# Attention of the later batches in fewer, longer visits to TensorE, with the transposed input loaded twice

## The chip, the cores and the metric

The kernel runs on one core of one Trainium2 chip. The metric is device time in microseconds (us): the median of 3 runs of the kernel before is 1649.5 us (1649.0 to 1649.99).

## The reference

Two stages follow each other. The first is an attention through 32 inducing points, for 4 batches of 12480 tokens with 128 channels; the second is a feed-forward layer over all 49920 tokens.

```python
def mab(q, kv):
    s = scale * (q @ kv.transpose(0, 2, 1))
    s = s - s.max(-1, keepdims=True)
    a = np.exp(s)
    a /= a.sum(-1, keepdims=True) + 1e-09
    return a @ kv

h = mab(inducing, x)          # 32 x 128 for each batch: every token is weighted
out = mab(x, h)               # 12480 x 128 for each batch: 32 scores a token
hid = out @ w_in              # 128 -> 2048
g = hid / (1 + exp(-1.702 * hid))
result = g @ w_out            # 2048 -> 128
```

All is float32, to float32 accuracy.

## The kernel before

**Tiling.** A batch is cut into super-blocks (`sups`, line 82): six of 4 x 512 tokens and a last one of 2 x 96; `NS` is 7. Attention works by super-block, the feed-forward layer by block of 512 tokens: 24 blocks for each batch, and one block for the rests of two batches together. Each block takes 8 steps (`NG`), one for each pair of 128-wide chunks of the 2048 hidden channels, so the main loop at line 751 has 784 steps.

**The feed-forward step.** `first(i)` (line 650) issues two 512-column products into `ph` (a PSUM pair, two of them in rotation), then ScalarE computes the gate `g`, ScalarE or VectorE a rounded copy `hi`, and VectorE the rest `lo`. `second(i, c)` (line 677) issues three products, hi with wl, lo with wh, hi with wh, into `pso`, for one of the two chunks: one half step. So a step is eight 512-column products. Half steps are issued late by `lag` halves; `lag` grows by one every `EXTRA` = 3 steps up to `LAG[1]` and is thrown back to `LAG[0]` = 6 when the attention yields `LUMP` (a run of exponentials on ScalarE with two loads of its function table); the halves over 6 are then issued at once, so TensorE has work while ScalarE is away. `ph_` holds the pairs hi and lo.

**The first layer's weights.** `hT` of a batch times `w_in` gives `hw[b, c]` for four quarters c (`h_w_in`, line 486): a product of TensorE, a copy of ScalarE, a subtraction of VectorE. The list `products` (line 727) says at which step each quarter is issued, counted from the first step that needs it: for batches 1 and 3 that is the block of rests. `phw` holds six such tiles. With them the feed-forward layer works on the attention's weights of a token (laid out as stacks `st` by `weights_of`, line 501, through DMA) and never builds the attention's output.

**The attention as a generator.** `attention(b)` (line 197) yields after each small piece; the main loop advances it by one piece a step (line 776), after the step's `first` and its halves. So whatever it issues to TensorE stands between two feed-forward steps: a visit. `hop(n)` and, in the later batches, `wait(n)` yield n times. For the batches 1 to 3 (`start` is false) its order is:

1. load the transposed input, one super-block a step (`load_xT`, line 158; 1 MB each): seven loads, six tiles `xt` in rotation (`px`) and one small tile `xt_last`;
2. `first_scores(s)` for each super-block: a visit of four 512-column products to the 32 columns of a quarter of the array each, which the trace records as eight; VectorE copies the scores from PSUM and reduces their maximum one step later; two more steps pass;
3. the maximum over the batch (`maximum`), then the exponentials of four super-blocks and a `LUMP`; the other three follow in the third super-block of item 4;
4. the weighted sum: for each of 25 pieces (`pieces`, 4 blocks of 32 x 4 tokens, 3 in the last) `load_x` (line 167) brings the untransposed input three pieces ahead in four DMAs of 64 KB, `weigh` (line 280) issues four products of 128 columns (eight in the trace) and two steps pass;
5. the normalisation gives `hT`;
6. `second_scores(s)` for each super-block, in two groups of 3 and 4: a visit like that of item 2 from the same `xt` tiles, VectorE's transpose and maximum, GpSimd's subtraction, and at the group's end the exponentials and a `LUMP`.

`full()` (line 133) holds the score visits back while no score tile is free; there are nine, given back by `aT_of` and `weights_of`.

**The first batch** (`start`) has no feed-forward work beside it. Its loads, scores, transposes (`turn_x`, line 180) and the splitting of the weights (`weights`, line 564) fill the first 70 us; five `xt` loads go out first, alternating with the four of `w_in`, and x4 is among them. In it the weighted sum already runs by whole super-blocks. Its second scores of super-blocks 2 to 6 fall into the main loop.

**Queues.** All DMAs are issued by SyncE in the order of the program: an instruction that waits there holds up all behind it, the stores of `outT` (line 775) and the stack tiles (line 541) among them. Every engine works its own instructions in program order.

Of the kernel before, what the change touches and what calls it, by code (L numbers as in the profile page):

```python
# [8 lines left out]
F32 = mybir.dt.float32  # L9
# [10 lines left out]
BLK = TOK // 32  # L20
XC = 4
RG = 2
LAG = 6, 10
EXTRA = 3
# [3 lines left out]
SPIN = 9, 20  # L28
ES = 5
FB = 5  # L30
LEAST = 2.0 ** -15
# [24 lines left out]
def set_attention_then_moe(ctx: ExitStack, tc, xT, x, indT, w_in, w_out, outT):  # L56
# [34 lines left out]
    const = ctx.enter_context(tc.tile_pool(name="const", bufs=1))  # L91
    px = ctx.enter_context(tc.tile_pool(name="px", bufs=NS - 1))
    pe = ctx.enter_context(tc.tile_pool(name="pe", bufs=EB))
    pt = ctx.enter_context(tc.tile_pool(name="pt", bufs=7))
    pst = ctx.enter_context(tc.tile_pool(name="pst", bufs=G))
    phw = ctx.enter_context(tc.tile_pool(name="phw", bufs=6))
    psm = ctx.enter_context(tc.tile_pool(name="psm", bufs=3))
# [34 lines left out]

    def full():
        return len(held) >= EB and not held[-EB]

# [30 lines left out]

    def load_x(b, s, c):

        t0, g, w = sups[s]
        n = min(XC, w // 32 - c * XC)  # L170
        t = pn.tile([P, XC, P], F32, tag="xn", name="xn")
        for j in range(g):
            r0 = b * N + t0 + j * w + c * XC * 32
            nc.sync.dma_start(
                t[32 * j:32 * j + 32, 0:n],
                x[r0:r0 + 32 * n, :].rearrange("(k i) c -> i k c", i=32),
            )
        return t
# [18 lines left out]
    def attention(b):  # L197
# [3 lines left out]
        if not start:  # L201
            for s in range(NS):
                load_xT(b, s)
                yield
# [7 lines left out]

        def first_scores(s):
            t0, g, w = sups[s]
            while s < NS - 1 and full():
                yield
            pa = ps_a.tile([P, 512], F32, tag="pa", name="pa")
            xg = xts[b, s][:, 0:g * w]
            if start:
                xg = xg.rearrange("c (k g i) -> c g k i", g=g, i=32)  # L220
            else:
                xg = xg.rearrange("c (g t) -> c g t", g=g)
            for j in range(g):
                pe_.matmul(
                    pa[32 * j:32 * j + 32, 0:w], indT_sb, xg[:, j], start=True, stop=True
                )
            yield
            q = 32 * g
            e, slot = take("s1", s)
            if start:  # L230
                act.copy(e[0:q, 0:w], pa[0:q, 0:w])
                dve.tensor_reduce(mx[0:q, s:s + 1], pa[0:q, 0:w], axis=AX.X, op=ALU.max)
            else:
                dve.tensor_copy(e[0:q, 0:w], pa[0:q, 0:w])
                dve.tensor_reduce(mx[0:q, s:s + 1], e[0:q, 0:w], axis=AX.X, op=ALU.max)
            s1[s] = e, slot

        def maximum(n):
# [40 lines left out]

        def weigh(pa, s, c, xn, i, n):  # L280

            t0, g, w = sups[s]
            q = 32 * g
            for kk in range(min(XC, w // 32 - c * XC)):
                j = i % G
                pe_.matmul(
                    pa[32 * j:32 * j + 32, 0:P], aTs[s][0:q, XC * c + kk, :], xn[0:q, kk],
                    start=(i < G), stop=(i >= n - G),
                )
                i += 1  # L290
            return i

        hu = psm.tile([P, P], F32, tag="hu", name="hu", bufs=1)
        rs1 = psm.tile([P, 1], F32, tag="rs1", name="rs1")
        pieces = [(s, c) for s in range(NS) for c in range(-(-sups[s][2] // (32 * XC)))]

# [3 lines left out]
        if start:  # L300

            turned = {}
            for s in range(ES):
                if s < 4:
                    squares()
                    fill(6 if s else 5)
                    if s < NS - ES:
                        load_xT(b, s + ES)
                yield from first_scores(s)
                if s > 0:  # L310
                    turned[s - 1] = turn_x(b, s - 1)
            squares()
            pace[0] = 1
# [9 lines left out]
            aT_of(4)  # L323
            turned[ES - 1] = turn_x(b, ES - 1)
            squares()
            fill(FILLS[0])
# [13 lines left out]
            for s in range(ES):  # L340
                for c in [c for r, c in pieces if r == s]:
                    i = weigh(
                        h1, s, c, turned[s][:, XC * c:], i, blocks(range(ES))
                    )
                if s == 0:
                    next(whole)
                    fill(FILLS[1])
                    next(whole)
                if s == 2:
                    next(whole)  # L350
                    fill(FILLS[2])
                    next(whole)
                    next(whole, None)
                if s == 1:
                    turned[ES] = turn_x(b, ES)
                    squares()
            nmx2 = found[0]
# [4 lines left out]
            for s in range(ES, NS):  # L362
                if s not in turned:
                    turned[s] = turn_x(b, s)
                for c in [c for r, c in pieces if r == s]:
                    i = weigh(
                        h2, s, c, turned[s][:, XC * c:], i, blocks(range(ES, NS))
                    )
            fill(FILLS[3])
# [9 lines left out]
        else:  # L379
            for s in range(NS):  # L380
                yield from first_scores(s)
                yield from wait(2)
# [5 lines left out]
            pa = ps_a.tile([P, 512], F32, tag="pa", name="pa")  # L388
            xq = pieces
            loaded = {}  # L390
            aT_of(0)
            for k in range(3):
                loaded[k] = load_x(b, *xq[k])
            yield from wait()
            i = 0
            for k, (s, c) in enumerate(xq):
                if c == 0 and s == 2:
                    for r in range(4, NS):
                        first_exponential(r, nmx)
                    yield LUMP  # L400
                if c == 1 and s + 1 < NS:
                    aT_of(s + 1)
                if k + 3 < len(xq):
                    loaded[k + 3] = load_x(b, *xq[k + 3])
                i = weigh(pa, s, c, loaded.pop(k), i, blocks(range(NS)))
                yield from wait(2)
            dve.tensor_copy(hu, pa[:, 0:P])
# [20 lines left out]

        def second_scores(s):

            t0, g, w = sups[s]
            q = 32 * g
            while s < NS - 1 and full():
                yield
            pa = ps_a.tile([P, 512], F32, tag="pa", name="pa")
            for j in range(g):
                pe_.matmul(
                    pa[32 * j:32 * j + 32, 0:w], hT[:, 0:M], xts[b, s][:, j * w:(j + 1) * w],
                    start=True, stop=True,
                )  # L440
            yield
            e, slot = take("e", s)
            k = w // 32
            e = e[:, 0:w].rearrange("p (k m) -> p k m", m=M)
            dve.transpose(e[0:q].rearrange("p k m -> p (k m)"), pa[0:q, 0:w])
            m2 = psm.tile([P, BLK], F32, tag="m2", name="m2")
            dve.tensor_reduce(m2[0:q, 0:k], e[0:q], axis=AX.X, op=ALU.max)
            yield
            eng = dve if start and s == 0 else nc.gpsimd
            eng.tensor_sub(e[0:q], e[0:q], m2[0:q, 0:k].unsqueeze(2).broadcast_to([q, k, M]))  # L450
            yield
            return e, slot
# [8 lines left out]
        if start:  # L461
            for s in range(2):
                mine[s] = yield from second_scores(s)
                exponentials(s, mine[s])
# [10 lines left out]
        yield  # L475
        turn = list(range(NS)) if b % 2 == 0 else [NS - 1, *range(NS - 1)]
        for some in (turn[2:],) if start else (turn[0:3], turn[3:]):
            yield from hop(20 if start else 8)
            for s in some:
                mine[s] = yield from second_scores(s)  # L480
            yield
            for s in some:
                exponentials(s, mine[s])
            yield LUMP
# [217 lines left out]
    with tc.tile_pool(name="pf", bufs=FB) as pf, tc.tile_pool(name="pw", bufs=2) as pw:  # L702
        dec = weights()
        for s in range(ES):
            if s < 4:
                load_w(w_in, s * WC)
            load_xT(0, s)
# [7 lines left out]
    po = ctx.enter_context(tc.tile_pool(name="po", bufs=2))  # L715
    pn = ctx.enter_context(tc.tile_pool(name="pn", bufs=4))

# [10 lines left out]
    for b in range(1, B):  # L728
        f = first_block[b, NS - 1 if b % 2 else 0] * NG
        products += [(f + at, b, c) for c, at in enumerate((-4, -2, 1, 3) if b % 2 else (-7, -5, -3, -1))]  # L730
    rest = attentions()
# [85 lines left out]
```

## Time and profile before

| | |
|---|---|
| time of the profiled execution | 1648.21 us |
| span inside it | 1646.4 us |
| median of 3 runs | 1649.5 us |
| TensorE matmul busy | 1609.2 us, 98% |
| VectorE busy | 1394.4 us, 85% |
| ScalarE busy | 1326.5 us, 81% |
| GpSimd busy | 202.4 us, 12% |
| DMA moved | 101.53 MB, mean 62 GB/s |

Matmuls are pipelined: a product of 512 columns is shown with some 400 ns while the next starts about 230 ns after it, so the busy time counts overlaps once and says only that TensorE is hardly ever idle. What a visit costs is therefore read from starts: from the start of one product to the start of the same product a few steps later. "x8" in a row is eight records merged; a score or weighing product in full float32 is recorded twice.

### The profile page before, as it was taken

Reading aid. Unit: us, or ns where it says so; the run is one execution under the profiler, and the core shown is the slowest. Engines: PE = TensorE matmul, PEld = TensorE weight load, DVE = VectorE, ACT = ScalarE, POOL = GpSimd, SP = SyncE. Lnnn points to the kernel's source line nnn. Section 1 sums busy time; section 2 is a strip of 40 time slices with the busy share of each in tenths; the row PEclk is TensorE's granted clock in tenths of the full one; section 3 lists DMA queues with packets and bytes.
Section 4 is the critical chain, followed back from the end, with each engine's and each line's share of the span. In section 5 each row is a group of like instructions: output and inputs, shape, how many; then the busy total and the mean of one; then the engine's idle time right before and its main releaser. Section 6 shows DMA issues by size and latency. Waiting matters only on the chain.

```text
span 1646.4 us, 22186 instructions
## 1 busy us (share of the span) xinstructions
PE 1609.2 (98%) x7737; PEld 1222.0 (74%) x7737; DVE 1394.4 (85%) x1526; ACT 1326.5 (81%) x1502; POOL 202.4 (12%) x134
## 2 busy tenths in 40 slices
PE   6799999999999999999999999999999999999999
PEld 4477777777777877777777777777777888888887
DVE  7798977878988898788988987877989888888886
ACT  6588788878887888878888778887788888888886
POOL 4321110102211011010120110110122001101100
PEclk9999999999999999999999999999999999999999
DMA  6105113311041112330105101322101011011010
GB/s 259 26 26 189 39 48 94 96 36 45 18 149 71 37 46 60 98 93 23 39 20 194 41 26 51 96 78 67 39 23 33 27 45 46 20 39 45 20 46 20
DMA packets 81950, 101.53 MB, mean 62 GB/s; under 512 B 14704, under 2 KB 53168, under 8 KB 78768
## 3 DMA queue, kind: packets, MB, share of 16 engines
q1 hardware_dynamic: 81840, 100.11, 19.5%
q8 instruction: 63, 1.03, 0.3%
q14 instruction: 47, 0.39, 0.1%
HBM read 48.94 MB, written 25.56 MB: 45 GB/s over the span
## 4 chain that ended last, share of the span: by engine, by line
PE 84%; DVE 3%; ACT 2%; issue 1%; DVEq 0%; ACTq 0%
PE pso L46 59%; PE ph L46 21%; PE pa L46 4%; DVE lo L46 2%; ACT g L46 1%; DVE hi L46 1%; ACT hi L46 0%; ACT L46 0%; DVE hw L46 0%; ACT e L46 0%; DVE sm L46 0%; ACT s L46 0%; DVE e L46 0%; ACT ob L46 0%; DVE m L46 0%
## 5 line engine op out<-in xcount | busy, mean ns | idle before, releaser
L46 DVE TENSOR_TENSOR lo<-g,hi 128x1024 fp32r<-128x1024 f32 (+1 forms) x784 | 985.4, 1266 | 155.6 <-ACT hi L46 142.0
L46 ACT ACTIVATE g<-ph 128x1024 f32<-128x1024 f32 (+1 forms) x784 | 804.1, 1029 | 258.5 <-PE ph L46 129.8
L46 PE MATMUL pso<-hi,wl 128*128 128x512 f32 (+1 forms) x1568 | 622.5, 397 | 0.0
L46 PE MATMUL pso<-hi,wh 128*128 128x512 f32 (+1 forms) x1568 | 616.2, 393 | 0.0
L46 PE MATMUL pso<-lo,wh 128*128 128x512 f32 (+1 forms) x1568 | 615.6, 393 | 0.0
L46 PE MATMUL ph<-st,hw 128*128 128x512 f32 x1536 | 495.9, 404 | 8.0 <-ACT g L46 4.4
L46 ACT ACTIVATE hi<-ph 128x1024 fp32r<-128x1024 f32 x453 | 462.6, 1021 | 0.0
L46 PEld LDWEIGHTS ph<-st,hw 128*128 128x128 f32 x1536 | 276.8, 188 | 117.5 <-ACT hi L46 27.2
L46 PEld LDWEIGHTS pso<-lo,wh 128*128 128x128 f32 x1568 | 293.9, 187 | 72.5 <-issue 2.4
L46 PEld LDWEIGHTS pso<-hi,wl 128*128 128x128 f32 x1568 | 294.4, 188 | 69.9 <-issue 2.9
L46 PEld LDWEIGHTS pso<-hi,wh 128*128 128x128 f32 x1568 | 294.3, 188 | 70.0
L46 DVE CAST hi<-g 128x1024 fp32r<-128x1024 f32 (+1 forms) x331 | 248.5, 751 | 65.0 <-ACT g L46 64.3
L513 POOL TENSOR_TENSOR e<-e,sm 128x512 f32<-128x512 f32 (+1 forms) x27 | 43.1, 1598 | 1164.2 <-DVE sm L46 922.1
L46 ACT COPY ob<-pso 128x512 f32<-128x512 f32 (+1 forms) x98 | 57.9, 590 | 21.5 <-PE pso L46 20.9
L450 POOL TENSOR_TENSOR e<-e,m 128x512 f32<-128x512 f32 (+1 forms) x27 | 49.7, 1840 | 163.5 <-DVE m L46 163.5
L517 POOL TENSOR_TENSOR e<-e,ah 128x512 f32<-128x512 f32 (+1 forms) x27 | 48.9, 1812 | 2.2
L46 PE MATMUL pa<-xt,indT_sb 128*32 128x512 f32 x192 | 28.2, 661 | 11.0 <-DMA xt<-in_xT 11.0
L46 ACT ACT_TABLE_LOAD x28 | 35.9, 1283 | 1.2 <-PEq L807 0.7
L46 PE MATMUL pa<-xn,aT 128*32 128x128 f32 (+1 forms) x594 | 31.9, 285 | 0.0
L46 PEld LDWEIGHTS pa<-xn,aT 128*32 128x32 f32 (+1 forms) x594 | 11.8, 107 | 26.9 <-issue 23.6
L516 POOL CAST ah<-e 128x512 fp32r<-128x512 f32 (+1 forms) x27 | 28.2, 1043 | 1.7
L46 PE MATMUL pa<-xt,hT 128*32 128x512 f32 x192 | 27.0, 641 | 1.0 <-DVE hT L46 1.0
(97 smaller groups left out, 436.0 us busy)
## 6 DMA issues: line engine op xcount, KB each, us to landing
xt<-in_xT SPq DMA_DIRECT2D x24, 1024.0 KB, 9.9
out_T<-ob SPq DMA_DIRECT2D x96, 256.0 KB, 2.0
xn<-in_x SPq DMA_DIRECT2D x288, 64.0 KB, 1.9
st<-ahT SPq DMA_DIRECT2D x192, 64.0 KB, 2.0
st<-alT SPq DMA_DIRECT2D x192, 64.0 KB, 2.0
raw<-in_w_in SPq DMA_DIRECT2D x4, 512.0 KB, 8.9
raw<-in_w_out SPq DMA_DIRECT2D x4, 512.0 KB, 12.5
xt_last<-in_xT SPq DMA_DIRECT2D x4, 96.0 KB, 10.8
```

The costliest lines, as they stand in the source:

```text
L46: return f(*a, **k)
L450: eng.tensor_sub(e[0:q], e[0:q], m2[0:q, 0:k].unsqueeze(2).broadcast_to([q, k, M]))
L513: eng.tensor_mul(e[0:q], e[0:q], sm[0:q, 0:nb].unsqueeze(2).broadcast_to([q, nb, M]))
L516: eng.tensor_copy(ah[0:q, 0:w], e2[0:q])
L517: eng.tensor_sub(e2[0:q], e2[0:q], ah[0:q, 0:w].bitcast(F32))
```

## The change

**The weighted sum goes by super-blocks.** `load_x(b, s)` brings a whole super-block of x (1 MB in four DMAs of 256 KB, two tiles in rotation), one super-block ahead; `weigh` issues all its 16 blocks in one visit, and six steps pass between visits instead of two. So 7 visits a batch take the place of 25.

**Scores go by pairs.** `first_scores` is split into `first_products` and `first_out`, `second_scores` into `second_products` and `second_out`. For the batches 1 to 3 two super-blocks' products are issued in one visit and their outputs follow two steps apart; `full(n)` asks for n free score tiles. The second scores' groups become 4 and 3. For batch 0 the pairs apply to the second scores of super-blocks 2 to 6.

**Four xt tiles** (`XB`) instead of six. Super-blocks 4 and 5 are loaded when the products of 0 and 1 are out; all six are loaded a second time (`again`) for the second scores, four during the weighted sum, two during the second scores. A later batch therefore starts with four loads in four steps, not seven in seven. In batch 0, x4 and x5 are loaded after the transposes of super-blocks 0 and 1.

**Smaller edits.** `LAG` is 6, 12 instead of 6, 10 and `ph_` one pair larger; `phw` has seven tiles; for batches 1 and 3 the products of `hT` with `w_in` are issued at steps -6, -4, -2, 1 instead of -4, -2, 1, 3. The hunks left out below are the rest of the split of `first_scores` and the two calls of `weigh` in batch 0.

```diff
@@ -18,15 +18,15 @@
 BLK = TOK // 32
-XC = 4
 RG = 2
-LAG = 6, 10
+LAG = 6, 12
 EXTRA = 3
 ES = 5
+XB = 4
 FB = 5
@@ -89,11 +89,11 @@
     const = ctx.enter_context(tc.tile_pool(name="const", bufs=1))
-    px = ctx.enter_context(tc.tile_pool(name="px", bufs=NS - 1))
+    px = ctx.enter_context(tc.tile_pool(name="px", bufs=XB))
     pe = ctx.enter_context(tc.tile_pool(name="pe", bufs=EB))
     pst = ctx.enter_context(tc.tile_pool(name="pst", bufs=G))
-    phw = ctx.enter_context(tc.tile_pool(name="phw", bufs=6))
+    phw = ctx.enter_context(tc.tile_pool(name="phw", bufs=7))
     psm = ctx.enter_context(tc.tile_pool(name="psm", bufs=3))
@@ -130,8 +130,9 @@

-    def full():
-        return len(held) >= EB and not held[-EB]
+    def full(n=1):
+
+        return any(len(held) + k >= EB and not held[len(held) + k - EB] for k in range(n))

@@ -164,16 +165,15 @@

-    def load_x(b, s, c):
+    def load_x(b, s):

         t0, g, w = sups[s]
-        n = min(XC, w // 32 - c * XC)
-        t = pn.tile([P, XC, P], F32, tag="xn", name="xn")
+        t = pn.tile([P, BLK, P], F32, tag="xn", name="xn")
         for j in range(g):
-            r0 = b * N + t0 + j * w + c * XC * 32
+            r0 = b * N + t0 + j * w
             nc.sync.dma_start(
-                t[32 * j:32 * j + 32, 0:n],
-                x[r0:r0 + 32 * n, :].rearrange("(k i) c -> i k c", i=32),
+                t[32 * j:32 * j + 32, 0:w // 32],
+                x[r0:r0 + w, :].rearrange("(k i) c -> i k c", i=32),
             )
@@ -199,7 +199,7 @@
         if not start:
-            for s in range(NS):
+            for s in range(XB):
                 load_xT(b, s)
...
@@ -235,6 +236,11 @@

+        def first_scores(s):
+            pa = first_products(s)
+            yield
+            first_out(s, pa)
+
         def maximum(n):
@@ -277,14 +283,14 @@

-        def weigh(pa, s, c, xn, i, n):
+        def weigh(pa, s, xn, i, n):

             q = 32 * g
-            for kk in range(min(XC, w // 32 - c * XC)):
+            for kk in range(w // 32):
                 j = i % G
                 pe_.matmul(
-                    pa[32 * j:32 * j + 32, 0:P], aTs[s][0:q, XC * c + kk, :], xn[0:q, kk],
+                    pa[32 * j:32 * j + 32, 0:P], aTs[s][0:q, kk, :], xn[0:q, kk],
                     start=(i < G), stop=(i >= n - G),
@@ -292,7 +298,16 @@
         rs1 = psm.tile([P, 1], F32, tag="rs1", name="rs1")
-        pieces = [(s, c) for s in range(NS) for c in range(-(-sups[s][2] // (32 * XC)))]
+        turn = list(range(NS)) if b % 2 == 0 else [NS - 1, *range(NS - 1)]
+
+        def pairs(some):
+            some = list(some)
+            return [some[k:k + 2] for k in range(0, len(some), 2)]
+
+        def again(s):
+
+            if s < NS - 1:
+                load_xT(b, s)

@@ -304,11 +319,13 @@
                     fill(6 if s else 5)
-                    if s < NS - ES:
-                        load_xT(b, s + ES)
+                if s == 0:
+                    load_xT(b, NS - 1)
                 yield from first_scores(s)
                     turned[s - 1] = turn_x(b, s - 1)
+                    if s - 1 + XB < NS - 1:
+                        load_xT(b, s - 1 + XB)
             squares()
@@ -322,6 +339,8 @@
             turned[ES - 1] = turn_x(b, ES - 1)
+            for s in range(XB - 1):
+                again(s)
             squares()
...
@@ -353,6 +369,7 @@
                     turned[ES] = turn_x(b, ES)
+                    again(XB - 1)
                     squares()
...
@@ -377,8 +391,16 @@
         else:
-            for s in range(NS):
-                yield from first_scores(s)
+            for pair in pairs(range(NS)):
+                while full(len(pair)):
+                    yield
+                pas = [first_products(s) for s in pair]
+                yield
+                for s, pa in zip(pair, pas):
+                    if s + XB < NS:
+                        load_xT(b, s + XB)
+                    first_out(s, pa)
+                    yield from wait(2)
                 yield from wait(2)
@@ -386,24 +408,24 @@
             pa = ps_a.tile([P, 512], F32, tag="pa", name="pa")
-            xq = pieces
-            loaded = {}
             aT_of(0)
-            for k in range(3):
-                loaded[k] = load_x(b, *xq[k])
+            xn = load_x(b, 0)
             yield from wait()
             i = 0
-            for k, (s, c) in enumerate(xq):
-                if c == 0 and s == 2:
+            for s in range(NS):
+                if s == 2:
                     for r in range(4, NS):
                     yield LUMP
-                if c == 1 and s + 1 < NS:
+                if s + 1 < NS:
                     aT_of(s + 1)
-                if k + 3 < len(xq):
-                    loaded[k + 3] = load_x(b, *xq[k + 3])
-                i = weigh(pa, s, c, loaded.pop(k), i, blocks(range(NS)))
-                yield from wait(2)
+                    later = load_x(b, s + 1)
+                i = weigh(pa, s, xn, i, blocks(range(NS)))
+                xn = later
+                yield from wait(3)
+                if s < XB:
+                    again(s)
+                yield from wait(3)
             dve.tensor_copy(hu, pa[:, 0:P])
@@ -426,19 +448,20 @@

-        def second_scores(s):
-
+        def second_products(s):
             t0, g, w = sups[s]
-            q = 32 * g
-            while s < NS - 1 and full():
-                yield
             pa = ps_a.tile([P, 512], F32, tag="pa", name="pa")
                 )
-            yield
+            return pa
+
+        def second_out(s, pa):
+
+            t0, g, w = sups[s]
+            q = 32 * g
             e, slot = take("e", s)
@@ -460,7 +483,11 @@
             for s in range(2):
-                mine[s] = yield from second_scores(s)
+                pa = second_products(s)
+                if s + XB < NS:
+                    again(s + XB)
+                yield
+                mine[s] = yield from second_out(s, pa)
                 exponentials(s, mine[s])
@@ -473,12 +500,18 @@
         yield
-        turn = list(range(NS)) if b % 2 == 0 else [NS - 1, *range(NS - 1)]
-        for some in (turn[2:],) if start else (turn[0:3], turn[3:]):
+        for some in (turn[2:],) if start else (turn[0:4], turn[4:]):
             yield from hop(20 if start else 8)
-            for s in some:
-                mine[s] = yield from second_scores(s)
-            yield
+            for pair in pairs(some):
+                while full(len(pair)):
+                    yield
+                pas = [second_products(s) for s in pair]
+                yield
+                for s, pa in zip(pair, pas):
+                    if s + XB < NS:
+                        again(s + XB)
+                    mine[s] = yield from second_out(s, pa)
+                yield from wait(2)
             for s in some:
@@ -701,9 +734,8 @@
         dec = weights()
-        for s in range(ES):
-            if s < 4:
-                load_w(w_in, s * WC)
+        for s in range(XB):
+            load_w(w_in, s * WC)
             load_xT(0, s)
@@ -713,7 +745,7 @@
     po = ctx.enter_context(tc.tile_pool(name="po", bufs=2))
-    pn = ctx.enter_context(tc.tile_pool(name="pn", bufs=4))
+    pn = ctx.enter_context(tc.tile_pool(name="pn", bufs=2))

@@ -727,7 +759,7 @@
         f = first_block[b, NS - 1 if b % 2 else 0] * NG
-        products += [(f + at, b, c) for c, at in enumerate((-4, -2, 1, 3) if b % 2 else (-7, -5, -3, -1))]
+        products += [(f + at, b, c) for c, at in enumerate((-6, -4, -2, 1) if b % 2 else (-7, -5, -3, -1))]
     rest = attentions()
```

## Rows read from the trace of the kernel before

**Rows 1.** The page's chain that ended last: shares of the span by engine.

```profile
PE 84%; DVE 3%; ACT 2%; issue 1%; DVEq 0%; ACTq 0%
```

**Rows 2.** TensorE's timeline, weighted sum of batch 1: start us, duration us, engine, line, products.

```profile
264.95 0.42 PE L46 MATMUL pa<-xn,aT 128*32 128x128 f32 x8
...
265.30 0.73 PE L46 MATMUL ph<-st,hw 128*128 128x512 f32 x2
...
267.27 0.62 PE L46 MATMUL ph<-st,hw 128*128 128x512 f32 x2
...
269.21 0.42 PE L46 MATMUL pa<-xn,aT 128*32 128x128 f32 x8
```

**Rows 3.** TensorE's timeline, first scores of batch 1.

```profile
175.73 1.07 PE L46 MATMUL pa<-xt,indT_sb 128*32 128x512 f32 x8
...
178.69 0.62 PE L46 MATMUL ph<-st,hw 128*128 128x512 f32 x2
...
180.54 0.63 PE L46 MATMUL ph<-st,hw 128*128 128x512 f32 x2
...
182.49 1.06 PE L46 MATMUL pa<-xt,indT_sb 128*32 128x512 f32 x8
```

**Rows 4.** TensorE's timeline, weighted sum of batch 0: one whole super-block.

```profile
42.62 1.08 PE L46 MATMUL h<-xf,aT 128*32 128x128 f32 x32
```

**Rows 5.** Timeline of weight loads, second scores of batch 0.

```profile
57.71 0.20 PEld L46 LDWEIGHTS pa<-xt,hT 128*32 128x32 f32 x4 [0.66 <-issue]
58.56 0.20 PEld L46 LDWEIGHTS pa<-xt,hT 128*32 128x32 f32 x4 [0.66 <-issue]
```

**Rows 6.** Stretches of 2 us: busy us (x count) by engine, PEclk, DMA share, GB/s.

```profile
58.00:60.00 2.00, 2.00 (x12) 0.20 (x4) 1.11 (x2) 0.00 (x0) 0.55 (x1) 0.50 0.00 0
16.00:18.00 2.00, 2.00 (x19) 0.99 (x17) 2.00 (x6) 2.00 (x3) 0.00 (x0) 1.00 1.00 408
486.00:488.00 2.00, 2.00 (x11) 1.62 (x11) 1.58 (x3) 2.00 (x4) 0.00 (x0) 1.00 1.01 422
```

**Rows 7.** Waits from 76 us on: waiter, releaser, us in total, times, longest us.

```profile
PE ph L46 <- DVE hw L46: 3.5, 3, 1.4
PE ph L46 <- ACT g L46: 3.5, 5, 1.2
PEld pa L46 <- DMA xn<-in_x: 2.2, 6, 0.4
```

**Rows 8.** TensorE's timeline at batch 1's quarters of hw.

```profile
470.20 1.04 PE L46 MATMUL pa<-w_in_sb,hT 128*128 128x512 f32 x2
...
476.39 0.58 PE L46 MATMUL ph<-left,hw 128*128 128x192 f32 x3 [1.12 <-DVE hw L46]
```

**Rows 9.** SyncE's timeline: first xn loads of batch 1, xt loads of batch 2.

```profile
224.58 5.66 SPq L174 DMA_DIRECT2D xn<-in_x  x12
...
481.25 2.35 SPq L164 DMA_DIRECT2D xt<-in_xT  x4
```

**Rows 10.** TensorE's timeline, first score visit of batch 2.

```profile
492.44 1.06 PE L46 MATMUL pa<-xt,indT_sb 128*32 128x512 f32 x8
```

**Rows 11.** DMA issue to landing: the xt loads from 470 to 490 us.

```profile
DMA to landing us min/median/max: 5.0/9.9/12.7
```

**Rows 12.** DMA issues by line from 478 to 495 us: count, KB each, median us to landing.

```profile
out_T<-ob SPq DMA_DIRECT2D x2, 96.0 KB, 7.8
```

**Rows 13.** The page's DMA issues, whole span: count, KB each, median us to landing.

```profile
out_T<-ob SPq DMA_DIRECT2D x96, 256.0 KB, 2.0
xn<-in_x SPq DMA_DIRECT2D x288, 64.0 KB, 1.9
```

**Rows 14.** Timeline of batch 0: transposes of x0, fifth score visit, maxima behind it.

```profile
13.93 2.86 PE L46 MATMUL ph<-ident,xt 128*128 128x128 f32 x16
...
23.47 1.07 PE L46 MATMUL pa<-xt,indT_sb 128*32 128x512 f32 x8
...
26.92 1.27 DVE L46 TENSOR_REDUCE mx<-pa 128x1 f32<-128x512 f32 x2
```

More of the change, by code (lines that the diff above doesn't have):

```diff
@@ L211, in attention, with first_products @@
         aTs = {}
-        def first_scores(s):
+        def first_products(s):
             t0, g, w = sups[s]
-            while s < NS - 1 and full():
-                yield
             pa = ps_a.tile([P, 512], F32, tag="pa", name="pa")
@@ L226, in first_scores, with first_out @@
                 )
-            yield
+            return pa
+        def first_out(s, pa):
+            t0, g, w = sups[s]
             q = 32 * g
@@ L340, in attention @@
             for s in range(ES):
[L341 to L344, printed above, removed]
+                i = weigh(h1, s, turned[s], i, blocks(range(ES)))
                 if s == 0:
@@ L364, in attention @@
                     turned[s] = turn_x(b, s)
[L365 to L368, printed above, removed]
+                i = weigh(h2, s, turned[s], i, blocks(range(ES, NS)))
             fill(FILLS[3])
@@ L427, in attention @@
             fill(3)
-        def second_scores(s):
+        def second_products(s):
             t0, g, w = sups[s]
-            q = 32 * g
-            while s < NS - 1 and full():
-                yield
             pa = ps_a.tile([P, 512], F32, tag="pa", name="pa")
@@ L440, in second_scores @@
                 )
-            yield
+            return pa
+        def second_out(s, pa):
+            t0, g, w = sups[s]
+            q = 32 * g
             e, slot = take("e", s)
@@ L475, in attention @@
         yield
-        turn = list(range(NS)) if b % 2 == 0 else [NS - 1, *range(NS - 1)]
-        for some in (turn[2:],) if start else (turn[0:3], turn[3:]):
+        for some in (turn[2:],) if start else (turn[0:4], turn[4:]):
             yield from hop(20 if start else 8)
-            for s in some:
-                mine[s] = yield from second_scores(s)
-            yield
+            for pair in pairs(some):
[8 more added lines that the diff above has]
+                yield from wait(2)
             for s in some:
```

## The prediction

> **What bounds the kernel now.** I read the chain of waits first: 84% of it is TensorE's own products and 3% VectorE [rows 1], so a microsecond taken out of TensorE's order after the first 75 us is a microsecond of the end. The waits from 76 us on say the same: TensorE stood still some 7 us, 3.5 for the quarters of hw and 3.5 for ScalarE's gate [rows 7]. The third view is TensorE's timeline, read from start to start. A step without a visit lasts 1.85 us (178.69 to 180.54, [rows 3]), eight products of 0.232. In the weighted sum two visits start 4.26 us apart (264.95 to 269.21, [rows 2]) with two steps between, so a visit of four blocks costs 4.26 - 3.70 = 0.56. In the scores two visits start 6.76 us apart (175.73 to 182.49, [rows 3]) with three steps between (one yield and `wait(2)`), so a visit costs 6.76 - 5.55 = 1.21.
>
> How much of that is work, and how much is coming and going? Two rows of batch 0 answer. One whole super-block of the weighted sum, 32 records, takes 1.08 us from the first start to the last end [rows 4], against 0.42 for eight [rows 2]: 24 more records cost 0.66, or 0.22 for eight. Four score products start 0.85 us apart (57.71, 58.56, [rows 5]) while the granted clock was 0.50, the 1.2 GHz level [rows 6]; eight take 1.71 there and 0.853 at the 2.4 GHz that the main loop is granted (1.00, [rows 6]). So both kinds of visit have the same surcharge: 0.56 - 0.22 = 0.34 and 1.21 - 0.85 = 0.36 us. It falls at the two changes between products that use the whole array and products that use a quarter.
>
> **The change part by part.**
>
> *Weighted sum.* Batches 1 to 3 have 18 whole super-blocks. Each had four visits, 4 x 0.56 = 2.24 us; it now has one of 0.56 + 0.66 = 1.22 us. Gain 1.02, times 18: 18.4 us. The last, small super-block keeps its one visit. Bounds: 0 if the surcharge belonged to the records and not to the visit, 18 x 3 x 0.56 = 30 if the added records were free; I take the rows of batch 0, which show the very shape.
>
> *Scores.* Per later batch 7 visits become 4 in the first scores and 7 become 4 in the second, in batch 0 five become three: 20 visits fewer, each 0.36: 7.2 us. Bounds 0 and 20 x 1.21 = 24; again the rate of rows 5 decides.
>
> *LAG 12.* Two half steps more are in hand at a LUMP: 2 x 3 x 0.232 = 1.39 us. The longest wait for ScalarE's gate is 1.2 us, the sum 3.5 in 5 [rows 7]; the three long ones should go. What may be late next is the regrowth: six short steps instead of four, in which TensorE asks for gates faster than on average. I take -3.0; bounds -4 and +4.
>
> *hw.* The waits on VectorE's hw are 3.5 us in three. In batch 1 the last quarter's product starts at 470.20 and the block of rests waits 1.12 us until 476.39 [rows 8], so the two engines behind it need 6.2 us. The quarters now go out two steps earlier, 3.7 us, or somewhat less where the steps are the shorter ones of the rests: more than the longest wait of 1.4. I take -3.5; bounds 0 and -3.9. The seventh tile lets the third quarter go out before the block of rests.
>
> *x by super-block.* SyncE issued 12 loads of 64 KB in 5.66 us [rows 9], 139 GB/s, and one lands 1.9 us after its issue [rows 13]. At that rate 1 MB is on chip after 7.5 + 1.9 = 9.4 us. It is asked for one visit ahead: 6 x 1.85 + 1.2 = 12.3 us. So it is hidden, with 2.9 us to spare, and the small waits for xn today (six of at most 0.4 us, of which the products feel a part, [rows 7]) go: -0.5, bounds -0.5 and +18 x 2.
>
> *Second loads.* 24 MB more in all, of which each reload has tens of microseconds until its second score; SyncE's wait in `again(4)` and `again(5)` is for products issued one step before. I cost them at 0; what they hide behind is the weighted sum, and without that cover each would cost one MB at 422 GB/s, 2.5 us [rows 6].
>
> *Four loads, then a pair.* Here the change adds a wait. Batch 2's loads are issued from 481.25 on, four in 2.35 us [rows 9], because a train of stack tiles stands before them on SyncE. The first visit came at 492.44 [rows 10], seven steps after the first load; now it comes four steps after it, about 492.44 - 3 x 1.85 = 486.9. It needs x0 and x1. x0 lands 5.0 us after its issue at the earliest [rows 11], at 486.3, and x1 one MB at 422 GB/s later, at 488.8. TensorE, and all feed-forward steps queued behind the visit, would wait 1.9 us. Batch 1 met no such train and batch 3 a shorter one: I take +3.0 for all, bounds 0 and +8.
>
> *Batch 0.* x4 is now loaded after the transposes of x0, which end at 13.93 + 2.86 = 16.8 us [rows 14]. DMA is full there at 408 GB/s [rows 6]; from about 2.5 us on that is 5.8 MB by then. Asked for before x4 are four tiles of w_in and two of w_out with 0.52 MB, four xt of 1.05 and `xt_last` with 0.1: 7.4 MB. So 1.6 MB are open, and x4 is through at 16.8 + 2.65/0.408 = 23.3 and usable, with the 1.9 us of a landing [rows 13], at 25.2. Its visit was at 23.47 and VectorE came to the two maxima only at 26.92 to 28.19 [rows 14]; the products end at 26.3 now, and a copy of ScalarE later the second maximum can run when VectorE comes to it. So VectorE's own queue hides the delay; the transposes behind the visit on TensorE may cost something: +0.5, bounds -0.5 and +3. x4 and x5 come again behind the scores of super-blocks 0 and 1, 2 MB or 5 us, while exponentials, weights and transposes still stand before the first stack tiles: 0.
>
> **Sum.** -18.4 - 7.2 - 3.0 - 3.5 - 0.5 + 3.0 + 0.5 = -29.1 us, from the profiled execution's 1648.2 to 1619.1. The median of the three runs lies 1.3 us above that execution; so 1620.4, or 1620.
>
> **A rule against it.** The longer visit is where the profile of before could mislead. The row of batch 0 has 32 weight loads and 32 products in 1.08 us [rows 4]: the loads pass beside the products. The Trainium skill (TensorE: Matmul & The Clock Gate, on packing small matmuls by row and column tiling) says that a weight load overlaps running products only where the row group differs, and these products all use all rows. By it the loads would stand alone in a long visit. With loads of 0.20 us in groups of four [rows 5], 0.05 each, 24 more would add some 1.2 us a super-block and take back 22 of the gain of 18.4: about 1642. The row contradicts it here, so it gets little.
>
> Transfers are the second place. In the burst of xt loads stores of 96 KB took 7.8 us to land [rows 12], where 256 KB take 2.0 as a rule [rows 13]: a small transfer waits for the large one ahead of it. The Trainium skill (DMA: Bandwidth & Descriptors, on queues, rings and completion order) says that each DMA engine takes a ring's descriptors in order, and all transfers here are issued on one queue; the trace agrees. That is the second rival's ground.
>
> **The rivals.**
>
> *Stack tiles behind the loads.* During the weighted sum 2 MB more stand in the ring ahead of stack tiles, up to 5 us at 422 GB/s. For it: the 7.8 us. Against it: no wait for a stack tile is among the waits of rows 7, though batches load 6 MB in a burst today. If one tile in each of 18 stretches came 0.8 us late: +14, about 1634. It would join a wait for x1 of up to 8.
>
> *ScalarE or VectorE takes over.* Both are near 85% busy; with TensorE faster they rise by under 2%. For it: the regrowth of the lag. If the longer lag adds waits instead of removing them, +4 for -3, and the pairs leave ScalarE empty and then crowd it: about 1630.
>
> *The visit has no fixed price.* If the surcharge came with the records, both large gains vanish and -29.1 becomes -3.5: 1646. Against it are rows 2 to 5, which agree on 0.34 and 0.36.
>
> *Slower: x comes late.* Place: the wait of `weigh` for xn, 18 times. It decides from 12.3 us after the request. If four loads of 256 KB do not stream but land as sixteen of 1.9 us in a row, x needs 30 us, TensorE waits 18 us at each visit, 18 x 18 = 324 us, about 1944; at 14 us the gain is gone (18 x 1.7 = 31). Against it: the 139 GB/s.
>
> **How the numbers follow.** Forecast 0.66, stack tiles 0.12, the two engines 0.08, the weight loads' rule 0.03, no fixed price 0.05, x late 0.06. The measurement tells 0.2%, 3.3 us, from no change. Faster by more: the first four and a part of the fifth, 0.90; within: 0.03; slower: 0.07. The forecast's own range is 1613 (all waits gone, none new) to 1628 (x1 at its upper bound, the longer lag without gain); to hold the time 8 times in 10 it takes in the stack tiles' 1634 with the upper bound of batch 0: 1612 to 1637.
>
> **What would show it.** Right: 18 weighing visits with 32 records, each 1.1 to 1.3 us; score visits with 16 records, about 2.06; waits on hw and on the gate below 2 us in all; a wait for xt of 1 to 2 us at the first pair of batches 2 and 3; the first stack product of batch 0 within 1 us of before; DMA near 126 MB. Wrong: waits of TensorE for xn or st in the weighted sum, waits for the gate above 5 us, or long visits that cost as much as four short ones.

## The result, and the profile after

| kernel | median of its runs, us | ratio to before (95%) | span of the profiled run, us |
|---|---|---|---|
| before | 1649.4 | 1 | 1646.4 |
| the change | 1656.4 | 1.0045 [1.0031, 1.0060] | 1654.6 |

The change made the kernel 7 us slower; 1620 was forecast. The page of the kernel after: span, busy time by engine, DMA, and the new x loads (count, KB each, median us to landing).

```profile
span 1654.6 us, 21847 instructions
...
PE 1595.2 (96%) x7737; PEld 1239.9 (75%) x7737; DVE 1382.3 (84%) x1524; ACT 1326.1 (80%) x1504; POOL 189.8 (11%) x134
...
DMA packets 81947, 126.66 MB, mean 77 GB/s; under 512 B 11632, under 2 KB 50096, under 8 KB 75696
...
xn<-in_x SPq DMA_DIRECT2D x72, 256.0 KB, 7.0
```

TensorE's busy time fell from 1609.2 to 1595.2 us and yet the end came later: the engine stood still more. Its waits from 76 us on (waiter, releaser, total, times, longest):

```profile
PE pa L46 <- DVE hw L46: 10.6, 6, 3.1
PE ph L46 <- ACT g L46: 7.9, 3, 2.7
PE pa L46 <- DVE e L46: 7.8, 5, 3.8
PE pa L46 <- DMA xt<-in_xT: 2.3, 1, 2.3
PE ph L46 <- ACT hi L46: 0.5, 2, 0.4
```

Some 7 us in [rows 7] have become 29. Waits of `pa` for `e` are new, and those of `pa` for `hw` too: score visits and quarters of hw that find both buffers of `pa` still being read. They sit in a few places, and TensorE's timeline shows the first (start, duration, line, products, [idle before <- releaser]):

```profile
181.86 0.40 PE L46 MATMUL pso<-hi,wh 128*128 128x512 f32 x1
182.19 1.92 PE L46 MATMUL pa<-xt,indT_sb 128*32 128x512 f32 x16
184.04 0.73 PE L46 MATMUL ph<-st,hw 128*128 128x512 f32 x2
184.62 0.40 PE L46 MATMUL pso<-hi,wl 128*128 128x512 f32 x1
...
243.55 0.36 PE L46 MATMUL pa<-xt_last,indT_sb 128*32 128x96 f32 x4
...
295.75 0.39 PE L46 MATMUL pso<-hi,wh 128*128 128x512 f32 x1
296.07 1.08 PE L46 MATMUL pa<-xn,aT 128*32 128x128 f32 x32
297.08 0.73 PE L46 MATMUL ph<-st,hw 128*128 128x512 f32 x2
297.65 0.39 PE L46 MATMUL pso<-hi,wl 128*128 128x512 f32 x1
...
411.12 1.03 PE L46 MATMUL pa<-xt,hT 128*32 128x512 f32 x6
413.14 1.97 PE L46 MATMUL pa<-xt,hT 128*32 128x512 f32 x16 [1.00 <-DVE e L46]
...
421.72 1.22 PE L46 MATMUL ph<-st,hw 128*128 128x512 f32 x2 [2.70 <-ACT g L46]
422.74 0.63 PE L46 MATMUL pso<-hi,wl 128*128 128x512 f32 x1
423.17 0.63 PE L46 MATMUL pso<-lo,wh 128*128 128x512 f32 x1
...
458.24 1.49 PE L46 MATMUL pa<-w_in_sb,hT 128*128 128x512 f32 x2 [3.05 <-DVE hw L46]
```

Read it in three parts. First, the visits themselves cost what was forecast. Around the long weighing visit: 295.75 to 297.08 is 1.33, less the product's own 0.23, and the next two products take 0.57 where 0.46 is usual: 1.21 us (1.22 forecast). Around the pair: 184.04 - 181.86 - 0.23, and 0.11 behind it: 2.06 us (2.06 forecast). Second, the last super-block's visit comes 61 to 62 us behind the pair of super-blocks 4 and 5, in every later batch. Before, in batch 1, it came 6.75 us behind super-block 5's:

```profile
189.24 1.06 PE L46 MATMUL pa<-xt,indT_sb 128*32 128x512 f32 x8
195.99 0.36 PE L46 MATMUL pa<-xt_last,indT_sb 128*32 128x96 f32 x4
```

Third, from 411 on two pairs of batch 1's second scores come back to back with no feed-forward step between (the second ends its wait at 413.14), then a wait of 2.70 us for the gate; the quarters of hw fall into the midst of the other second scores (3.05 us at 458.24).

### The profile page after: what moved, and what is told of

It is laid out like the page before. It is cut to its first block, busy times and chain, and to the rows that moved or that the text cites. A ratio compares the mean times of both kernels' runs of the same rounds, so it can differ in the third digit from the quotient of the medians.

```text
span 1654.6 us, 21847 instructions
## 1 busy us (share of the span) xinstructions
PE 1595.2 (96%) x7737; PEld 1239.9 (75%) x7737; DVE 1382.3 (84%) x1524; ACT 1326.1 (80%) x1504; POOL 189.8 (11%) x134
## 4 chain that ended last, share of the span: by engine, by line
PE 89%; DVE 5%; ACT 2%; DMA 2%; issue 1%; POOL 1%; SPq 0%; ACTq 0%; DVEq 0%; POOLq 0%
PE pso L46 63%; PE ph L46 22%; PE pa L46 4%; DVE lo L46 2%; DMA xt<-in_xT 2%; DVE e L46 1%; DVE m L46 1%; ACT hi L46 1%; ACT g L46 1%; DVE hw L46 0%; DVE hi L46 0%; ACT L46 0%; DVE t L46 0%; ACT s L46 0%; DVE sm L46 0%
## 5 line engine op out<-in xcount | busy, mean ns | idle before, releaser
L46 PE MATMUL ph<-st,hw 128*128 128x512 f32 x1536 | 490.9, 401 | 11.1 <-ACT g L46 8.9
L46 PEld LDWEIGHTS ph<-st,hw 128*128 128x128 f32 x1536 | 284.2, 189 | 99.3 <-issue 16.4
L46 DVE CAST hi<-g 128x1024 fp32r<-128x1024 f32 (+1 forms) x329 | 242.2, 736 | 86.3 <-ACT g L46 85.6
L546 POOL TENSOR_TENSOR e<-e,sm 128x512 f32<-128x512 f32 (+1 forms) x27 | 39.1, 1448 | 1143.5 <-DVE sm L46 898.4
L473 POOL TENSOR_TENSOR e<-e,m 128x512 f32<-128x512 f32 (+1 forms) x27 | 34.8, 1289 | 203.2 <-DVE m L46 203.2
L549 POOL CAST ah<-e 128x512 fp32r<-128x512 f32 (+1 forms) x27 | 34.5, 1277 | 1.7
L46 ACT ACTIVATE e<-e 128x512 f32<-128x512 f32 (+1 forms) x28 | 15.2, 576 | 21.6 <-POOL e L473 14.0
L46 PE MATMUL pa<-w_in_sb,hT 128*128 128x512 f32 x24 | 14.0, 669 | 12.1 <-DVE hw L46 8.3
```

Of the source, the lines that this page charges most:

```text
L46: return f(*a, **k)
L546: eng.tensor_mul(e[0:q], e[0:q], sm[0:q, 0:nb].unsqueeze(2).broadcast_to([q, nb, M]))
L549: eng.tensor_copy(ah[0:q, 0:w], e2[0:q])
```

## The cause, and the experiments

In the diff, `while s < NS - 1 and full()` became `while full(len(pair))`. The first form lets the last, small super-block pass: `take` (line 136) gives it a tile of its own and no place in `held`. The second form counts it. With nine tiles, six of them just taken by this batch, it waits for tiles of the batch before, which `weights_of` gives back only as the feed-forward layer reaches their super-blocks, 32 steps (59 us) apart. **Theory A:** that wait makes the attention late (by some 25 steps of 1.85 us: 243.55 here, 196.58 in e1 below); when the layer needs its stack, `lay_out` (line 743) draws the missing pieces from the generator at one stroke, with no steps between. Counted from the program's order there are 16, 12 and 16 such pieces at three places, 18, 14 and 18 in e2 below, and none in the kernel before, in e1, e3 and e4. The `LUMP` among them is thrown away with the rest, so no halves go out ahead of the exponentials. **Rival B:** four `xt` tiles and the second loads are to blame: transfers come late, or SyncE holds up the stack tiles.

**e1: the wait counts only super-blocks that take a tile.**

```diff
-                while full(len(pair)):
+                while full(sum(s < NS - 1 for s in pair)):
```

(both places).

> The changed kernel, but the wait for free score tiles counts only the super-blocks that take one: the last, small one takes none. Theory A (the small super-block's needless wait makes each later batch's attention some 30 steps late, and its second scores are then issued in a rush with no feed-forward work between): the last first-score visit of batch 2 comes about 13 us after the pair before it instead of 62, no two score visits of different pairs stand back to back, the waits of TensorE on VectorE's e (7.8 us) and hw (10.6 us) fall below 2 us in all, and the time is 1614 to 1626 us. Rival B (the four loads before a pair, the second loads and the pairs themselves hold TensorE up): the stalls stay, 1645 us or more.

1629.67 us, ratio 0.9866 [0.9851, 0.9881]. Without that wait the change is 27 us faster by the medians, 29.5 by the ratios; theory A holds, though the time is 3.7 us above the upper end expected. TensorE's timeline of e1 has the small visit 15 us behind the pair, and what is left of rival B:

```profile
181.55 1.92 PE L46 MATMUL pa<-xt,indT_sb 128*32 128x512 f32 x16
196.58 0.36 PE L46 MATMUL pa<-xt_last,indT_sb 128*32 128x96 f32 x4
...
478.79 1.07 PE L46 MATMUL pa<-xt,indT_sb 128*32 128x512 f32 x8 [0.70 <-DMA xt<-in_xT]
482.44 1.94 PE L46 MATMUL pa<-xt,indT_sb 128*32 128x512 f32 x8 [2.58 <-DMA xt<-in_xT]
...
872.71 1.07 PE L46 MATMUL pa<-xt,indT_sb 128*32 128x512 f32 x8 [0.79 <-DMA xt<-in_xT]
```

**e2: the wait alone, in the kernel before.**

```diff
-            while s < NS - 1 and full():
+            while full():
```

(both places).

> The kernel before, with one edit: its last, small super-block too waits for a free score tile. Theory A: the attention of each later batch comes some 30 steps later, the second scores are rushed as in the changed kernel, and 25 to 40 us are lost: 1675 to 1690 us. Rival B: the wait is harmless by itself, 1650 us.

1680.32 us, ratio 1.0158 [1.0133, 1.0184]. The wait by itself, with none of the rest of the change, costs 26 us by the ratio and 29 by the medians. Timeline of e2: the small visit, now 55 us behind the one before it instead of 6.75; and its waits from 76 us on, the kinds that the kernel after has:

```profile
191.57 1.07 PE L46 MATMUL pa<-xt,indT_sb 128*32 128x512 f32 x8
246.51 0.36 PE L46 MATMUL pa<-xt_last,indT_sb 128*32 128x96 f32 x4
```

```profile
PE pa L46 <- DVE hw L46: 10.0, 4, 3.5
PE ph L46 <- ACT g L46: 8.6, 6, 2.6
PE ph L46 <- DVE hw L46: 3.9, 2, 2.0
PE pa L46 <- DVE e L46: 2.7, 3, 1.0
```

**e3: the condition left as changed, more tiles.** Twelve score tiles (`LAG` 6, 10 makes room).

```diff
-LAG = 6, 12
+LAG = 6, 10
-    EB = NS + 2
+    EB = NS + 5
```

> The changed kernel with 12 score tiles instead of 9, and LAG 6, 10 instead of 6, 12 to make room; the condition is left as it is. With 12 tiles the small super-block's wait is met early. Theory A: no rush, 1615 to 1630 us. Rival B: as the changed kernel or slower, 1655 us.

1620.39 us, ratio 0.9809 [0.9794, 0.9823]. So it is the tiles that the wait is for (the `LAG` edit by itself makes no difference that can be told, e5 below). Timeline of e3, the small visit back at 15 us:

```profile
182.64 1.92 PE L46 MATMUL pa<-xt,indT_sb 128*32 128x512 f32 x16
197.77 0.36 PE L46 MATMUL pa<-xt_last,indT_sb 128*32 128x96 f32 x4
```

**e4: e1, and three steps between the four loads and the first pair.**

```diff
+            yield from hop(3)
```

> The first run's kernel with three more steps between the four loads of a later batch and its first pair of scores, so that the first visit comes seven steps after the first load, as in the kernel before. The prediction's term for the loads was +3 us over all batches: in the first run TensorE should wait 2 to 3 us for xt at the first pair of batch 2 and up to 1.5 at batch 3, and here not at all; 2 to 4 us faster than the first run. If the loads are no matter: the same time.

1621.97 us, ratio 0.9820 [0.9805, 0.9834]: 7.7 us less than e1, twice to four times what was expected. The rows of e1 show 4.1 us of waits for `xt`, and behind the longest of them TensorE's granted clock was for a part of the time at its lower level (0.60 over a stretch of 2 us). That stretch of e1 (columns as in the last section), then the waits of e4 from 76 us on, none for `xt`:

```profile
484.00:486.00 2.00, 2.00 (x10) 1.51 (x7) 0.00 (x0) 0.44 (x1) 0.00 (x0) 0.60 0.67 279
```

```profile
PE ph L46 <- ACT hi L46: 1.8, 5, 0.6
PE ph L46 <- ACT g L46: 1.1, 1, 1.1
PE pa L46 <- DVE hw L46: 0.3, 1, 0.3
```

All waits of e4 come to 3.2 us and those of e1 to 7.7 (4.1 for `xt`, 1.6 for hi, 1.3 for g, 0.7 for hw). With 1.7 for the clock (worked out in the last section) that is an estimated 6.2 us, against 5.9 between the two spans (1626.3 and 1620.4).

The ratios split the change into three: e4 -0.0180, the loads +0.0046 (e1 less e4), the wait +0.0179 (the change less e1); in us of 1649.4: -29.7, +7.6, +29.5. They add up to the ratio of the change by construction, so that is no check; the check of the wait is e2, which doesn't start from the change.

The next four start from e4 and take one of its gains away. They ran beside other runs of the kernel before than e1 to e4 did (medians from 1649 to 1652 us), so a difference to e4 below 3 us says nothing.

**e8: the weighted sum in four visits a super-block again.** x still loaded by super-block; `weigh` takes a range of blocks.

```diff
-                i = weigh(pa, s, xn, i, blocks(range(NS)))
+                for k0 in range(0, sups[s][2] // 32, 4):
+                    i = weigh(pa, s, xn, i, blocks(range(NS)), k0, k0 + 4)
+                    if k0 < 8:
+                        yield
+                    ...
```

> The fourth run's kernel with the weighted sum of a whole super-block cut into four visits of four blocks, one or two steps apart; the loads of x and all else stay by whole super-blocks. Term of the prediction: 54 more visits at 0.34 us, so 18.4 us slower than the fourth run, with 8 records and about 0.56 us a visit. Rival (no fixed price of a visit): same time.

1641.39 us, ratio 0.9950 [0.9935, 0.9965]: 19.4 us more than e4 by the medians, 21.4 by the ratios, where 18.4 was expected. The four short visits' price comes back in full.

**e6: hw at the old steps, six tiles.**

```diff
-... (-6, -4, -2, 1) if b % 2 else ...
+... (-4, -2, 1, 3) if b % 2 else ...
-    phw = ctx.enter_context(tc.tile_pool(name="phw", bufs=7))
+    phw = ctx.enter_context(tc.tile_pool(name="phw", bufs=6))
```

> The fourth run's kernel with the old steps of the quarters of hw in batches 1 and 3 (-4, -2, 1, 3) and six tiles for them. The prediction's term is -3.5 us: this run should lose 3 to 4 us against the fourth, with TensorE waiting some 3.5 us for VectorE's hw in two or three places. Rival: TensorE, less delayed by other things, meets the quarters elsewhere, and it loses under 1 us.

1626.27 us, ratio 0.9862 [0.9846, 0.9877]: 4.3 us more than e4 by the medians, 6.9 by the ratios (3 to 10 by their intervals), 3.4 by the spans (1623.8 and 1620.4). The wait that had gone is back, with the size it had in [rows 7]:

```profile
PE ph L46 <- DVE hw L46: 3.4, 4, 1.5
```

**e5: `LAG` 6, 10 again.**

> The fourth run's kernel with LAG 6, 10 as before. The prediction gave the longer lag -3.0 us (bounds -4 and +4): if that holds, this run loses 2 to 4 us against the fourth, which was 29.2 us faster than before. Rival, from the waits of the third run, which had LAG 6, 10 and only 2.4 us of waits on ScalarE in all: the longer lag is worth less than 1.5 us, and its regrowth puts back part of what it takes.

1623.02 us, ratio 0.9839 [0.9826, 0.9853], span 1620.2: 1.0 us more than e4 by the medians, 3.1 by the ratios, none by the spans; no difference that can be told.

**e7: score visits of one super-block, three steps apart** (20 visits more).

```diff
-            return [some[k:k + 2] for k in range(0, len(some), 2)]
+            return [some[k:k + 1] for k in range(0, len(some), 1)]
```

and the `wait(2)` behind each pair taken out.

> The fourth run's kernel with every score visit of the later batches, and the second scores 2 to 6 of batch 0, for one super-block, three steps apart as in the kernel before. Term of the prediction: 20 more visits at 0.36 us, so 7 us slower than the fourth run, with 8 records and about 1.2 us a visit. Rival (no fixed price of a visit): same time.

1621.72 us, ratio 0.9834 [0.9818, 0.9851]: a miss, the pairs seem worth nothing. Read from starts, the visits of e7 do cost 6.5 us more than e4's, near the 7 forecast; but e7 shows no wait of TensorE from 76 us on at all, where e4 has the 3.2 us above. The other 3.3 us can hide in the measurement: e7 less e4 is 2.3 by the ratios, -1 to 6 by their intervals. What spares e7 its waits is told by e11.

**e9 and e10: all together, with 12 tiles and `LAG` 6, 10; e10 with single visits.**

> Everything together: the wait that counts only the super-blocks that take a tile, three steps between the four loads and the pair, and 12 score tiles instead of 9 (which leaves room for a stack that lies 10 steps back and not 12). If tiles coming free (theory A) is no longer what holds the scores once the last super-block passes freely, the extra tiles are worth 0 to 2 us: 1619 to 1623 us beside the 1622 to 1623 of the runs with 9 tiles. If the first full super-blocks still wait for tiles in a way that costs (the rival), 12 tiles are worth 3 to 5 us more: 1616 to 1619. No wait for transposed x above 1 us after the first 76 us in either case.

> The same with every score visit a single super-block, three steps apart (20 more visits). If the pairs' saving of some 0.3 us a visit is all given back as waits on ScalarE and VectorE behind them, as the two runs with 9 tiles say: within 3 us of the pairs' time. If the saving comes through where tiles are plentiful: 5 to 7 us slower than the pairs. The profile should show, from 76 us on, no waits of TensorE on g and hi with single visits, and some 3 us of them with pairs.

e9 1620.7 us, ratio 0.9828 [0.9814, 0.9843]; e10 1628.79 us, 0.9881 [0.9865, 0.9897]. Here the pairs are worth 8 us, though the waits of the two for g and hi hardly differ (3.1 us with pairs, 2.9 with single visits; none was expected with single ones). The extra tiles add nothing to e4. e3 has neither the mended condition nor the three steps and is as fast, with 2.5 us of waits for `xt` left. Part of the reason is in its rows: behind that wait the granted clock stayed at 1.00 (last section), so e1's 1.7 us for the clock are not paid there, and the two waits of 0.70 and 0.79 are gone. Even so e3 has 1.7 us more of waits than e4 and a span 1.6 us shorter; the runs of e3 themselves lie 2 us apart (1618.7 to 1620.8), and the rest stays open.

**e11: e7 with `LAG` 6, 10**, to tell tiles from `LAG`.

> Single score visits three steps apart with 9 score tiles, as in the run at 1621.7 us, but with a stack that lies 10 halves back and not 12. With 12 tiles and 10 halves the same visits took 1628.8 us. If the two halves made that difference (theory: single visits come more evenly, and with 12 halves in hand the gates of ScalarE are always ready): 1627 to 1630 us, with 2 to 4 us of waits of TensorE on g and hi from 76 us on. If the number of tiles made it (rival: with more tiles the attention's pieces run ahead and crowd ScalarE): 1620 to 1623 us and waits below 0.5 us.

1629.92 us, ratio 0.9865 [0.9849, 0.9882]: it was `LAG`. Three of e11's waits for the gate come at the first exponentials of batches 1 to 3:

```profile
234.09 0.73 PE L46 MATMUL ph<-st,hw 128*128 128x512 f32 x2 [1.20 <-ACT g L46]
...
629.58 0.73 PE L46 MATMUL ph<-st,hw 128*128 128x512 f32 x2 [1.19 <-ACT g L46]
...
1017.15 0.73 PE L46 MATMUL ph<-st,hw 128*128 128x512 f32 x2 [1.19 <-ACT g L46]
```

and so they do before, the first of them shorter:

```profile
232.67 0.73 PE L46 MATMUL ph<-st,hw 128*128 128x512 f32 x2 [0.72 <-ACT g L46]
...
633.11 0.73 PE L46 MATMUL ph<-st,hw 128*128 128x512 f32 x2 [1.19 <-ACT g L46]
...
1025.91 0.74 PE L46 MATMUL ph<-st,hw 128*128 128x512 f32 x2 [1.19 <-ACT g L46]
```

With nine tiles the four combinations are, by ratio: single visits and 10 halves 0.9865, single and 12 0.9834, pairs and 10 0.9839, pairs and 12 0.9820. Either edit takes these three waits away (neither e7 nor e5 has one above 0.3 us on the gate; the one of 1.1 us in e4 lies elsewhere, in batch 2's second scores), so the second finds less to take. In time, both together make 7.4 us, by intervals 4 to 11; each on top of the other 2 or 3 us, which the intervals don't tell from nothing.

No version tried beats e4 by more than the measurement tells; e3, e4, e7 and e9, at 1620 to 1622 us, are the best.

## Why the prediction was wrong, step by step

**The step that failed** is the one on scores: "Per later batch 7 visits become 4 in the first scores and 7 become 4 in the second". It priced what a visit costs TensorE and took when it comes as given. The condition in front of the visits was in the diff, and in the text of the kernel before ("holds the score visits back while no score tile is free"); that `s < NS - 1` had gone, and that the last visit would now wait for the batch before, was not read. The part of the prediction that lists added waits names only the loads. None of the rivals had a wait in the order of the program, one that no engine's semaphore shows: in the profile it is no wait at all, only a visit that comes late (243.55), and 170 us later a crowd. The prediction's sign of being wrong, waits for the gate above 5 us, did come (7.9), but not by the rival that it belonged to. Price: 29.5 us as taken out of the change (e1), 26 as put into the kernel before (e2). Where it went can be estimated from rows: TensorE's waits are 29.1 us in the kernel after and 7.7 in e1, and its clock fell six times against once after the start, at 1.7 us each (last section); 21.4 and 8.5 make 29.9, against 28.3 between the spans.

**Four loads, then a pair** (+3.0, bounds 0 to +8): place and sign right. For batch 2, e1 has 0.70 and 2.58 us where 1.9 was forecast, and 0.79 for batch 3. The price was 7.6 by ratio and 5.9 by span, inside the bounds but mis-sized; the loss of clock behind the long wait was in no term.

**Weighted sum** (-18.4): right. 1.21 us a visit, and 19.4 us back in e8. So the rival without a fixed price is out. So is the rival of the weight loads: 24 more records in a visit cost 0.65 us (1.21 less 0.56, [rows 2]), and not 1.2 us more. That 1.2 was the prediction's estimate by the rule in the Trainium skill (TensorE: Matmul & The Clock Gate, on packing small matmuls by row and column tiling); it was too high in itself, since the 0.05 us a load came from a stretch at half clock. In the long visit the 32 loads pass in 0.81 us, 0.025 each:

```profile
296.07 0.81 PEld L46 LDWEIGHTS pa<-xn,aT 128*32 128x32 f32 x32 [0.36 <-issue]
```

A load and its product together cost 0.027 us (0.65 for 24), so the loads don't stand alone: next to nothing would be left for the products.

**hw** (-3.5): right, 3.4 us of waits and of span in e6; the times alone (4.3 by medians, 6.9 by ratio) agree, but are wider.

**Scores and `LAG`** (-7.2 and -3.0): not simply to be added, since the same three waits go with either (e11). Alone, the pairs are worth 4.3 us (e11 less e5, by ratio) or 8.7 with twelve tiles (e10 less e9), `LAG` 5.1 (e11 less e7); together 7.4 (4 to 11) where the sum had 10.2. The prediction read the waits for the gate once, for `LAG`, and did not ask whether the pairs would take them away too.

**x by super-block, second loads, batch 0**: no wait for `xn` or `st` stands among TensorE's waits after 76 us, though 256 KB take 7.0 us to land. The rivals of late x and of stack tiles behind the loads are out. The first stack product of batch 0 is within 0.4 us of its old place, 70.39 before:

```profile
70.39 1.36 PE L46 MATMUL ph<-st,hw 128*128 128x512 f32 x4 [1.90 <-DMA st<-alT]
```

and 70.79 after:

```profile
70.79 1.27 PE L46 MATMUL ph<-st,hw 128*128 128x512 f32 x4 [0.82 <-DVE hw L46]
```

e1 is the change as the prediction meant it. It gives 22.1 us by ratio where the sum had 29.1, so without the step that failed the forecast would still have been 7 us too low. The loads cost 4.6 more than their term, and the overlap of scores and `LAG` would account for 2.8, though the intervals don't pin that down. That e4's 1622 lies beside the forecast 1620 is luck: e4 has three steps more, and its loads cost nothing.

## What to carry to other kernels

When a diff rewrites a loop's guard, list for each value of the loop which condition held it before and which holds it now, and for each resource asked for, who gives it back and how many steps later; a generator that waits by yielding leaves no wait in the profile. Two edits that aim at the same row of waits are priced together. When a change loses where its parts should gain, look in the timeline for a visit that has moved before looking for one that has grown.

## What was not expected of the hardware

TensorE's clock can fall behind a long wait. Stretches of 1 and 2 us of the kernel after, around the 2.70 us wait (length, busy us and count of PE, PEld, DVE, ACT, POOL; granted clock; DMA share; GB/s):

```profile
419.00:421.00 2.00, 0.02 (x1) 0.00 (x0) 0.00 (x0) 1.97 (x3) 0.00 (x0) 1.00 0.11 45
421.00:422.00 1.00, 0.28 (x1) 0.28 (x2) 0.30 (x1) 1.00 (x2) 0.00 (x0) 0.66 0.00 0
422.00:424.00 2.00, 2.00 (x5) 1.55 (x6) 1.93 (x4) 2.00 (x3) 0.00 (x0) 0.50 0.00 0
424.00:426.00 2.00, 2.00 (x9) 1.61 (x8) 1.97 (x4) 0.65 (x2) 1.58 (x2) 0.82 0.00 0
```

While TensorE stands still the row says 1.00; as it starts again it is granted 0.50, the 1.2 GHz level, and products start 0.43 us apart (422.74 to 423.17) instead of 0.23. The stretch from 424 to 426 has a part at either level (0.82). The three stretches from 421 on lose 0.34, 2 x 0.50 and 2 x 0.18, some 1.7 us in all.

The length of the wait alone doesn't decide. Of the eight waits above 2 us in the kernel after, six (2.26 to 3.85 us) were followed by a clock of 0.50, and two were not: one of 2.20 us, and one of 2.70 us that ended at 1232.10, as long as the one above:

```profile
1232.00:1234.00 2.00, 1.90 (x8) 1.49 (x9) 1.89 (x3) 2.00 (x4) 0.00 (x0) 1.00 0.00 0
```

In e3 a wait of 2.51 us for `xt`, which ended at 484.14, had no such sequel either, nor had the waits of 1.19 us in e11. The stretch of e3, and of e11 behind one of its waits:

```profile
484.00:486.00 2.00, 1.86 (x12) 0.89 (x13) 0.00 (x0) 0.10 (x1) 0.00 (x0) 1.00 1.00 406
```

```profile
629.00:631.00 2.00, 1.42 (x6) 1.20 (x7) 1.41 (x2) 2.00 (x3) 0.00 (x0) 1.00 1.15 230
```

What decides between them stays open.
